# Attention products recorded ahead of the first turned tokens in a fused attention, Fourier and MLP kernel

## The chip, the cores and the metric

The kernel runs on one core of one Trainium2 chip. The metric is the time of one execution on the device in microseconds (us), the median of several runs. All data are float32.

## The reference

Four inputs matter: `q`, `k`, `v` of shape (4, 8, 768, 64), a decay `lam` for each of 8 heads, and two weights of shapes (512, 2048) and (2048, 512). Cut to what matters, the program computes this:

```python
# attention with a decay, in blocks along the sequence, state kv of 64 x 64 for each head
intra = ((qb @ kb.T) * Dmask) @ vb            # Dmask[i,j] = lam**(i-j) for i >= j, else 0
inter = (qb * lam_pow) @ kv
out[block] = intra + inter
kv = lam_block * kv + (kb * rev_pow).T @ vb
# (B,H,S,D) -> (B,S,H*D), then the second half
mixed = real(fft(fft(x, axis=1), axis=2))     # along the sequence and along the width
u = x + mixed
un = (u - mean(u)) / sqrt(var(u) + 1e-6)      # over the width of 512
out = u + maximum(un @ w_ch1, 0) @ w_ch2
```

## The kernel before, in words

The kernel works in chunks of 128 tokens, 6 for each of the 4 batches. Each part of the work is a Python generator that records instructions and yields a number, its estimate of how long they take. The function `beside` weaves two generators: it advances the second one in proportion to what the first has yielded. So the numbers decide in which order instructions are recorded. After that a scheduler of the language orders the instructions of each engine again, by what it takes to be ready and by the recorded order. An instruction handed to `tc.keep_in_program_order` is pinned: it stays behind everything that was recorded before it on its engine.

These are the parts, with the lines that the profile shows:

- `attn(b)` is the attention of one batch, chunk by chunk. `attn_in` loads k, q and v (L263, on the SyncE queue), and turns k and q on TensorE (L274, L279), copied back by ScalarE (L276, L281). VectorE makes `qs`, q times its decay (L285). `attn_out` multiplies k and q (L298), and VectorE applies the decay mask to give `sc` (L302, twice). It then updates the state (L315 to L320, not in the last chunk), adds `qs` times the old state (L328) and `sc` times v (L332) in one accumulation, and copies the result as `oT` (L335). Last, `oT` is turned to tokens (L348) and copied (L352, L353). In the last chunk of batch 1, two gathers of mirrored tokens (`mirror_a`, L439 and L445) are recorded after L302, and two more (`mirror_b`, L452) at its end.
- `fft_ln(b)` does the Fourier mix and the norm of one batch. VectorE folds mirrored rows together (L426 to L484), so that the transforms are products with small cosine and sine tables. TensorE multiplies along the sequence (L516), then along the width (L529 to L534) for three groups of 2 x 128 tokens. ScalarE and VectorE put the results together (L592 to L600; for the first row of one group also L606 to L609). `norm` then takes the statistics (L546, L547 on VectorE; L550, L551 on GpSimd), writes the normalised tokens `un` (L564, two halves for each of two tiles, one buffer), turns them on TensorE (L569) and copies them to `ut` on ScalarE (L570).
- `mlp(b, g, f0, f1)` multiplies `ut` with the first weight (L633), applies the maximum (L639 on VectorE or L641 on ScalarE), multiplies with the second weight (L647), and adds to the tokens (L654, L655 or L658, L659). Four of the twelve groups (`PLAIN`) go this way, three of them in two halves of the hidden width. The others (`late`, L720 to L796) follow at the end with a scheme of seven products in place of eight.
- `weights()` loads weight blocks as raw words (L209, on the SyncE queue, 512 KB each) and turns them into float32 with VectorE and ScalarE passes (L216 to L225). The raw blocks share four buffers with the hidden activations `hr`.

The change sits where batch 0's mix is woven with batch 1's attention and the weights:

```python
run(beside(part(mix, T_FOLD), T_FOLD, att1, 3.25 * t_chunk))
run(beside(mix, 24.0, beside(att1, 2.75 * t_chunk, w, 0.16 * NW), 0.16 * NW + 1.75 * t_chunk))
```

`mix` is `fft_ln(0)`. When `norm` of its first group yields 5.0 after the statistics, the weave advances `att1` and `w` for that long, and then the normalised tokens and their turning are recorded.[...]

## Time and profile before

| | |
|---|---|
| median of 3 runs | 826.14 us (825.62 to 828.82) |
| profiled execution | 824.8 us from the first instruction to the last |
| TensorE busy | 798.2 us (97%) |
| TensorE weight loads | 637.5 us (77%) |
| VectorE busy | 437.8 us (53%) |
| ScalarE busy | 186.5 us (23%) |
| GpSimd busy | 78.4 us (10%) |
| data moved | 68.88 MB |

In the profile PE is TensorE, PEld its weight load, DVE VectorE, ACT ScalarE, POOL GpSimd, and SPq the SyncE queue. A row of a timeline gives start and length in us, the engine, the source line, the operation, output and input tiles with their sizes, and the number of records. In brackets stands how long the engine had been idle before, and what ended that. A product of float32 operands shows as two records. The page divides the span into 40 slices of 20.6 us and gives the busy share of each engine in tenths, and with PEclk the TensorE clock that was granted. The weave with the change runs from 76 to 115 us. It is followed by the first half of the MLP beside the front of batch 1; the seven-product part begins at about 434 us and lasts to the end.

### The profile page before, as it was taken

The page shows a single profiled execution, that of the slowest core. Times are in us where ns is not written, and L with a number is a line of the kernel's source. Part 1 is how long each engine was busy: PE and PEld are TensorE (multiplying, and loading weights), DVE is VectorE, ACT ScalarE, POOL GpSimd, SP SyncE. Part 2 cuts the span into 40 slices and gives each one's busy share as a digit, 9 for nine tenths or more (in the row PEclk, how much of TensorE's full clock was granted, in tenths as well). Part 3 has the DMA queues.
Part 4 walks back from the last instruction along what each step waited for, and adds up shares of the span by engine and source line. Part 5 has one row for each costly group of instructions (what it writes and reads, how often), then busy time and mean ns, then how long its engine had stood idle before and what let it go on. Part 6 is the DMA issues. An engine that isn't in the chain of part 4 may idle for free.

```text
span 824.8 us, 11701 instructions
## 1 busy us (share of the span) xinstructions
PE 798.2 (97%) x4608; PEld 637.5 (77%) x4608; DVE 437.8 (53%) x1018; ACT 186.5 (23%) x448; POOL 78.4 (10%) x102
## 2 busy tenths in 40 slices
PE   7989799999999999999999999999999999999998
PEld 5767675758575857768748888888888888888886
DVE  6899779685745571345895541155313561146311
ACT  3755243324521211212102210022001220012100
POOL 3123310011110110220100000000000000000000
PEclk9999899999999999999999999999999999999999
DMA  9969343238842137530442011100111001110010
GB/s 240 259 132 280 98 152 99 83 75 202 212 116 68 55 74 141 128 120 2 115 115 89 1 52 51 52 1 0 54 50 52 0 1 39 33 33 0 1 39 25
DMA packets 126684, 68.88 MB, mean 84 GB/s; under 512 B 111150, under 2 KB 112174, under 8 KB 126630
## 3 DMA queue, kind: packets, MB, share of 16 engines
q1 hardware_dynamic: 121488, 55.67, 26.6%
q0 software_dynamic: 2112, 6.69, 2.5%
q10 hardware_dynamic: 3030, 5.78, 2.0%
q8 instruction: 36, 0.59, 0.3%
q14 instruction: 18, 0.15, 0.1%
HBM read 48.72 MB, written 19.40 MB: 83 GB/s over the span
## 4 chain that ended last, share of the span: by engine, by line
PE 81%; DVE 9%; issue 4%; DMA 3%; ACT 2%; POOL 1%; POOLq 0%; ACTq 0%; DVEq 0%; SPq 0%
PE p L767 23%; PE p L720 23%; PE pm L647 10%; PE pm L633 8%; PE pa L332 3%; PE pa L298 3%; PE pa L516 3%; PE pa L328 2%; DMA raw<-in_moe_w_ch_dram 2%; PE pa L274 1%; PE pa L315 1%; PE pa L348 1%; PE pa L279 1%; DMA x<-xb,ix 1%; DVE sc L302 1%
## 5 line engine op out<-in xcount | busy, mean ns | idle before, releaser
L633 PE MATMUL pm<-ut,w 128*128 128x256 f32 x512 | 119.9, 383 | 0.0
L647 PE MATMUL pm<-w,hr 128*128 128x512 f32 x256 | 115.8, 597 | 0.6 <-DVE w L225 0.6
L633 PEld LDWEIGHTS pm<-ut,w 128*128 128x128 f32 x512 | 94.2, 190 | 15.8 <-issue 4.1
L720 PE MATMUL p<-ur,w 128*128 128x256 f32 x384 | 93.8, 379 | 0.0
L647 PEld LDWEIGHTS pm<-w,hr 128*128 128x128 f32 x256 | 46.7, 190 | 50.0 <-issue 47.8
L720 PEld LDWEIGHTS p<-ur,w 128*128 128x128 f32 x384 | 73.0, 190 | 10.3 <-issue 0.5
L720 PE MATMUL p<-us,w1s 128*128 128x256 f32 x256 | 65.7, 379 | 0.0
L767 PE MATMUL p<-w,hs 128*128 128x256 f32 x256 | 58.0, 379 | 0.5 <-DVE y L788 0.5
L767 PE MATMUL p<-w2s,hs 128*128 128x256 f32 x256 | 57.9, 379 | 0.0
L767 PE MATMUL p<-w,ha 128*128 128x256 f32 x256 | 57.9, 379 | 0.0
L767 PEld LDWEIGHTS p<-w,hs 128*128 128x128 f32 x256 | 48.5, 190 | 7.5 <-DVE y L788 0.9
L767 PEld LDWEIGHTS p<-w2s,hs 128*128 128x128 f32 x256 | 48.6, 190 | 6.6
L767 PEld LDWEIGHTS p<-w,ha 128*128 128x128 f32 x256 | 48.6, 190 | 6.6
L720 PEld LDWEIGHTS p<-us,w1s 128*128 128x128 f32 x256 | 48.6, 190 | 6.6
L747 ACT COPY ha<-p 128x256 f32<-128x256 f32 x32 | 11.9, 372 | 169.1 <-PE p L720 139.4
L622 POOL DMA_INDIRECT out_dram<-y,ix x12 | 11.8, 988 | 402.4 <-DVE y L793 341.6
L758 DVE TENSOR_TENSOR ha<-p,ha 128x256 f32<-128x256 f32 x32 | 13.6, 425 | 45.2 <-ACT ha L757 45.2
L298 PEld LDWEIGHTS pa<-qT,kT 64*128 64x128 f32 x384 | 26.8, 198 | 12.8 <-ACT qT L281 6.7
L302 DVE TENSOR_TENSOR sc<-pa,decay 128x512 f32<-128x512 f32 x48 | 31.5, 683 | 8.2 <-PE pa L298 8.2
L332 PE MATMUL pa<-sc,v 128*64 128x128 f32 x384 | 32.3, 286 | 3.1 <-DVE sc L302 3.0
L298 PE MATMUL pa<-qT,kT 64*128 64x128 f32 x384 | 31.5, 297 | 2.9 <-ACT qT L281 2.6
L720 PE MATMUL p<-us,w 128*128 128x256 f32 x128 | 32.9, 379 | 0.0
(144 smaller groups left out, 1122.1 us busy)
## 6 DMA issues: line engine op xcount, KB each, us to landing
raw<-in_moe_w_ch_dram SPq DMA_DIRECT2D x32, 512.0 KB, 4.6
k<-in_k_dram SPq DMA_DIRECT2D x24, 256.0 KB, 5.0
q<-in_q_dram SPq DMA_DIRECT2D x24, 256.0 KB, 5.9
v<-in_v_dram SPq DMA_DIRECT2D x24, 256.0 KB, 4.9
ud<-x SPq DMA_DIRECT2D x16, 256.0 KB, 2.3
utd<-e SPq DMA_DIRECT2D x64, 64.0 KB, 2.2
u<-ud SPq DMA_DIRECT2D x16, 256.0 KB, 2.7
ur<-utd SPq DMA_DIRECT2D x6, 512.0 KB, 4.4
```

The costliest lines, as they stand in the source:

```text
L298: mm(pss[hi][:, hp, :], lhsT=kT[HD[hi], hp, :], rhs=qT[HD[hi], hp, :], start=True, stop=True)
L302: nc.vector.tensor_tensor(t, pss[hi], decay[:, hi::2, :], op=ALU.mult)
L328: mm(po[HD[hi], hp, :], lhsT=s_old[HD[hi], hp, :], rhs=qs[HD[hi], hp, :], start=(hp == 0), stop=False, skip_group_check=True)
L332: mm(po[HD[hi], hp, :], lhsT=vt[:, 2 * hp + hi, :], rhs=sc[hi][:, hp, :], start=(c == 0 and hp == 0), stop=(hp == HP - 1), skip_group_chec ...
L516: mm = nc.tensor.matmul(ps[0:m, n, :], lhsT=piece(a, i, n), rhs=cs[0:rows, a, i in (2, 3), n, :], start=(a == 0), stop=(a == 1))
L622: nc.gpsimd.indirect_dma_start(out=out.rearrange("b s d -> (b s) d"), out_offset=row_of(2 + HC * (b + 1) + T - HC), in_=y[:, :], in_offset ...
L633: nc.tensor.matmul(ps, lhsT=w1[:, c, 128 * fc:128 * fc + 128], rhs=ut[:, c, :], start=(c == 0), stop=(c == KO - 1))
L647: nc.tensor.matmul(ps, lhsT=hr[(fc - f0) // 4][:, fc % 4, 128 * i:128 * i + 128], rhs=w2[:, fc, :], start=(fc == f0), stop=(fc == f1 - 1))
L720: nc.tensor.matmul(ps, lhsT=s2.A[a][:, kt, 128 * i:128 * i + 128], rhs=U[b][:, kt, :], start=(first and kt == 0), stop=(kt == 1), skip_gro ...
L747: nc.scalar.copy(a11, two(X))
L758: V.tensor_tensor(a22, two(Z), a22, op=ADD)
L767: nc.tensor.matmul(ps, lhsT=h[a][:, s, i, :], rhs=s2.B[b][:, i, :], start=(first and i == 0), stop=(i == HF - 1), skip_group_check=True)
```

## The change

Two edits, both in `norm` and both for the first group of batch 0, `PLAIN[0]`. The number yielded after the statistics becomes 9.0, so that more of batch 1's attention is recorded between the statistics and the tokens. And the very first turning product is pinned on TensorE behind all that was recorded before it, so that the scheduler doesn't move it ahead of these attention products. It is meant to give TensorE the attention's products while VectorE and GpSimd work on the norm.

```diff
-            yield 5.0 if (b, g) == PLAIN[0] else 1.0
+            yield 9.0 if (b, g) == PLAIN[0] else 1.0
...
                 if plain:
                     pt = psum_a([128, KO, 128])
                     for c in range(KO):
-                        nc.tensor.transpose(pt[:, c, :], un[:, 128 * c:128 * c + 128], ident)
+                        mm = nc.tensor.transpose(pt[:, c, :], un[:, 128 * c:128 * c + 128], ident)
+                        if (b, g, i, c) == (*PLAIN[0], 0, 0):
+
+                            tc.keep_in_program_order(mm)
                     nc.scalar.copy(ut[:, :, 128 * i:128 * i + 128], pt)
```

Lines behind the first edit keep their numbers; those behind the second are three higher in the changed kernel (L633 becomes L636).

## The prediction

> **What bounds the kernel now.** I read the page's busy shares and slices first, then the table of stretches around the one dip, the timelines of TensorE, VectorE and the SyncE queue there, and last the waits of TensorE after it.

> ```profile
> PE   7989799999999999999999999999999999999998
> PEclk9999899999999999999999999999999999999999
> ```
> TensorE is the bound nearly everywhere. The fifth slice (82 to 103 us) is the only one in which the granted clock falls.

> ```profile
> 88.00:92.00 4.00, 0.26 (x3) 0.02 (x1) 3.07 (x8) 1.05 (x4) 1.29 (x2) 1.00 1.09 245
> 92.00:96.00 4.00, 2.94 (x13) 2.57 (x14) 2.06 (x5) 0.86 (x2) 1.66 (x2) 0.52 0.26 87
> 96.00:100.00 4.00, 4.00 (x37) 3.65 (x38) 2.00 (x5) 0.81 (x4) 1.48 (x2) 0.63 0.55 162
> ```
> Columns: stretch, then busy time of TensorE, weight load, VectorE, ScalarE, GpSimd, then granted clock. TensorE does nothing for most of 88 to 92, and is granted half its clock just after.

> ```profile
> 87.66 0.60 PE L348 MATMUL pa<-ident,oT 128*128 128x128 f32 x4
> 92.55 1.09 PE L569 MATMUL pa<-ident,un 128*128 128x128 f32 x4 [4.29 <-DVE un L564]
> 94.15 0.69 PE L569 MATMUL pa<-ident,un 128*128 128x128 f32 x2 [0.51 <-DVE un L564]
> 97.33 1.93 PE L298 MATMUL pa<-qT,kT 64*128 64x128 f32 x16
> 99.19 1.09 PE L328 MATMUL pa<-qs,st 64*64 64x128 f32 x16
> 102.26 1.09 PE L332 MATMUL pa<-sc,v 128*64 128x128 f32 x14
> 115.12 0.67 PE L569 MATMUL pa<-ident,un 128*128 128x128 f32 x4 [0.43 <-DVE un L564]
> 135.14 1.12 PE L647 MATMUL pm<-w,hr 128*128 128x512 f32 x2 [0.56 <-DVE w L225]
> ```
> The turned tokens (L569) wait 4.29 us for the first normalised tokens. The attention products of the last chunk of batch 1 (L298, L328, L332) stand behind them, although their inputs were there.

> ```profile
> 89.75 0.65 DVE L285 TENSOR_TENSOR qs<-pa,qpow 128x512 f32<-128x512 f32 x1
> 90.42 0.65 DVE L224 SCALAR_TENSOR_TENSOR w<-raw,w 128x512 f32<-128x512 uint32 x1
> 91.99 0.74 DVE L564 TENSOR_SCALAR un<-x,mv,rs 128x256 f32<-128x256 f32 x2 [0.93 <-POOL rs L551]
> 97.97 0.43 DVE L596 TENSOR_TENSOR ds<-pa,bs 128x256 f32<-128x256 f32 x1 [3.56 <-ACT bs L592]
> ```
> ```profile
> 103.38 0.37 SPq L263 DMA_DIRECT2D v<-in_v_dram  x1
> 103.85 1.04 SPq L209 DMA_DIRECT2D raw<-in_moe_w_ch_dram  x2
> 115.97 0.33 SPq L209 DMA_DIRECT2D raw<-in_moe_w_ch_dram  x1
> ```
> VectorE idles 3.56 us because TensorE is late. The load of v waits for L332 to free its buffer, and the raw weights (L209) queue behind that load.

> ```profile
> PE pa L516 <- DVE fe L475: 2.2, 3, 1.0
> PE pa L332 <- DVE sc L302: 1.6, 1, 1.6
> PE p L767 <- DVE y L788: 0.5, 1, 0.5
> ```
> These are all of TensorE's named waits from 160 us to the end: 4.3 us. What TensorE gains before 150 us should therefore reach the end.

> [...]

> **The change part by part.** In the changed program's instruction order only TensorE, VectorE and ScalarE differ, and only between the rows that ran at 88 and about 146 us. No instruction is added or removed. TensorE: L298, L328 and L332 now stand before L569, and L348 (turning oT) before the first L633. VectorE: both L302 and one L225 stand before the first L564, and some weight and fold work (L217 to L225, L426 to L430) moves up from after 112 us. The two edits of the diff (9.0 for 5.0, and the pin) bring about one order; I cost that order. I replay it with durations of this trace at full clock; spacings back to back are 0.60 us for a 512-wide VectorE pass, 0.34 for a 256-wide one, and 0.44 for one L633 product (two records of 0.22).

> 1. *The gap.* qT is ready at 88.49 (copy of 0.59 from 87.90). L298 runs 88.6 to 89.8 (1.16 in its full-clock rows, against 1.93 here). L328 waits for qs, 90.40, and runs 90.5 to 91.6. On VectorE L224 ends its slot at 91.02; L302 twice, to 92.3. L332 starts on the first at 91.8, waits for the second at 92.4, and is done by 93.4. So 3.3 us of products (1.16 + 1.09 + 1.09) go into the 4.29 us gap, in pieces: the idle spells are 0.3, 0.75, 0.2 and 0.4 us.
> 2. *What is put behind.* L564 follows L302 and L225: 91.02 + 1.20 + 0.60 = 92.8 instead of 91.99, so the first L569 goes at 93.4 instead of 92.55, about when L332 ends. Queued behind the added waits on TensorE are these transposes; VectorE's second L564, ScalarE's ut copies and all of the first group's norm wait for them. That is a loss of 0.85 us, and the only one I find.
> 3. *The clock.* [...] Between 48 and 52 us TensorE was busy 3.02 of 4.00 and kept its clock. I take full clock; then L569 and L529 to L534 run at 0.22 us a product, not 0.43. The second un starts at 94.1, its transposes at 94.7, L534 ends at 96.3, L348 at 96.6, and L633 starts at 96.6. In the trace L348 and the products up to 103.28 without three L633 stand at 103.28 + 0.44 - 1.3 = 102.4. TensorE is 5.8 us ahead there. Of this 2.7 us are clock (0.5 + 0.3 + 0.2 on the transposes, 5 x 0.21 on L529 to L534, 0.77 on L298, rounded), the rest the filled gap.
> 4. *The next norm.* The VectorE chain starts at 96.9 instead of 97.97 and no longer holds L302 (1.2 us): L596 to L600, 1.9; L546 and L547, 1.5; GpSimd's two, 1.2. So L564 starts at 101.5 instead of 103.83. TensorE has ten L633 (4.4 us) until 101.0, then waits 1.1 us for L569, where before it waited for nothing. After L530 to L532 it is 105.7 us with 12 L633 done; in the trace 108.81 with 8. Lead: 3.1 + 4 x 0.44 = 4.9 us.
> 5. *VectorE until 135.* Here VectorE limits: from 108.3 it idles 1.1 us until 135. Its idle spells from 90 to 135 sum to 10.2 us (0.93, 0.35, 3.56, 1.17, 0.76, 2.26, 0.92, 0.22). In the replay they sum to 5.3 (0.6, 2.0, 1.2, 0.4, 0.3, 0.6, 0.2). It can use that time because v and the raw weights behind it are issued at 93.5 and 94.0 instead of 103.38 and 103.85; a raw block landed 4.4 us after its issue at 115.97, so both are in by 102 even beside the gathers. The third raw block follows the first L224, at 104.7 instead of 115.97. Two short passes (0.67) move behind the third block's L225, which ends at 135.08 - 4.9 - 0.67 = 129.5.
> 6. *Down products.* L647 starts at 116.1 instead of 121.10; its 28 records and two L633 take it to 129.0; it waits for L225 until 129.6 instead of 135.14. One L633 moved behind it: lead 5.6 - 0.4 = 5.2 us.
> 7. *The gathers.* L352 waits for L609 and its successors: 110.7 instead of 111.95. With the same 7 us to the landed gather (issue 112.63, first L452 at 114.96, landing 3.7 us later) the fold's input is in at 117.7, wanted at 118.4. This is hidden by 0.7 us.

> From there the order is the old one and TensorE has next to no waits: 826.14 - 5.2 = 820.9 us.

> **The rivals.** *A: the clock still falls,*[...]. For: the pieces fill only about 60% of 88 to 94. Against: 48 to 52 us. Then the 2.7 us of step 3 are lost: gain 2.5, 823.6 us; a late fold (step 7) or a weight wait gives about the same. *B: VectorE gives it all back.* For: L647 waits for L225 already, and VectorE is busy without a break from 115 to 135. If the raw blocks don't come earlier, L225 stays at 135.08 and the time at 826. Against: their only blocker in the queue is v's buffer, which L332 frees. *C: slower.* The pin puts the first norm behind L332, and the clock falls under it: +0.85 of step 2, and 1.8 us more for L298, L328 and L332 at half clock before the transposes, 828.8 us. For: the norm is a chain, and the chain of waits runs through it. Against: TensorE would still have done 3.3 us of work that it now does later.

> **How the numbers follow.** Forecast (gain 4 to 6.5): 0.74. A: 0.14. B: 0.06. C: 0.06. Half a per cent is 4.1 us; nearly all of the forecast lies above it, some just below: faster 0.70, same 0.24, slower 0.06. The range runs from 819.0 (the whole 5.8 us and half of the 2.3 us of waits that steps 4 and 1 leave) to 824.3, past A; B, C and the tails make up the rest.

> **What would show it.** Right: L569 starts near 93.4 with a short wait; the clock is 1.00 in 92 to 100; v is issued near 93.5; TensorE waits about 1.1 us before the second norm's L569; the last pair of L647 waits for L225 near 129.6; after 150 us everything is about 5 us earlier. Wrong: a clock near 0.5 after 92; L225 of the third block after 131; L426 waiting for the second gather for more than a us; or a lead at 150 us that is gone at the end.

## The result, and the profile after

The changed kernel takes 821.45 us (median of 6 runs, 820.58 to 823.3), the kernel before beside it 825.81 us (6 runs, 825.07 to 828.82). The ratio is 0.9945, with a 95% interval of 0.9927 to 0.9962: a gain of 4.4 us by the medians. A second series gave 822.27 against 826.99 us (ratio 0.996, 0.9941 to 0.9979). The profiled execution spans 819.4 us, before 824.8.

The page's slices of the changed kernel, busy share and granted clock:

```profile
PE   6989899999999999999999999999999999999998
PEclk9999999999999999999999999999999999999999
```

The fifth digit of PEclk, the only low one before, is now 9. The table of stretches, with the columns in the order of before (TensorE, weight load, VectorE, ScalarE, GpSimd, then the granted clock, the busy share of the DMA engines and GB/s; `pa` and `pm` in the rows that follow are the kernel's two pools of buffers for products, `pa` of the attention and the mix, `pm` of the MLP):

```profile
88.00:92.00 4.00, 2.82 (x36) 2.15 (x38) 4.00 (x10) 0.59 (x3) 1.30 (x2) 1.00 1.20 283
92.00:96.00 4.00, 3.49 (x34) 2.97 (x33) 2.03 (x5) 1.78 (x4) 2.15 (x2) 1.00 0.58 149
96.00:100.00 4.00, 4.00 (x22) 3.56 (x21) 3.45 (x8) 0.99 (x5) 0.99 (x1) 1.00 0.95 319
```

TensorE works 2.82 us of the first stretch, where it worked 0.26, and the clock stays at 1.00 where it was 0.52 and 0.63. The timeline of TensorE in the changed kernel:

```profile
87.20 0.60 PE L348 MATMUL pa<-ident,oT 128*128 128x128 f32 x4
88.09 1.16 PE L298 MATMUL pa<-qT,kT 64*128 64x128 f32 x16 [0.29 <-ACT qT L281]
90.00 1.09 PE L328 MATMUL pa<-qs,st 64*64 64x128 f32 x16 [0.75 <-DVE qs L285]
91.26 0.43 PE L332 MATMUL pa<-sc,v 128*64 128x128 f32 x2 [0.17 <-DVE sc L302]
91.86 1.09 PE L332 MATMUL pa<-sc,v 128*64 128x128 f32 x14 [0.17 <-DVE sc L302]
92.88 0.67 PE L569 MATMUL pa<-ident,un 128*128 128x128 f32 x4
...
101.74 0.67 PE L569 MATMUL pa<-ident,un 128*128 128x128 f32 x4 [1.04 <-DVE un L564]
...
129.40 1.12 PE L650 MATMUL pm<-w,hr 128*128 128x512 f32 x2 [0.17 <-DVE w L225]
...
147.63 0.76 PE L569 MATMUL pa<-ident,un 128*128 128x128 f32 x4 [0.94 <-DVE un L564]
```

The wait of 4.29 us is gone. In its place stand the three products with short waits, and the first turned tokens go out behind them without any. The same kernel's VectorE and SyncE queue:

```profile
92.33 0.73 DVE L564 TENSOR_SCALAR un<-x,mv,rs 128x256 f32<-128x256 f32 x2
96.52 0.43 DVE L599 TENSOR_TENSOR ds<-pa,bs 128x256 f32<-128x256 f32 x1 [1.96 <-ACT ds L598]
128.66 0.68 DVE L225 SCALAR_TENSOR_TENSOR w<-w,e 128x512 f32<-128x512 f32 x1
```

```profile
92.98 0.37 SPq L263 DMA_DIRECT2D v<-in_v_dram  x1
93.45 11.54 SPq L209 DMA_DIRECT2D raw<-in_moe_w_ch_dram  x3
```

VectorE's longest wait has fallen from 3.56 to 1.96 us, and v and the raw weights leave some 10 us earlier. The third raw block of that row is issued at 104.66, before at 115.97. TensorE's named waits from 155 us to the end are those of before:

```profile
PE pa L516 <- DVE fe L475: 2.1, 3, 1.0
PE pa L332 <- DVE sc L302: 1.6, 1, 1.6
PE p L770 <- DVE y L791: 0.5, 1, 0.5
```

**How the gain is measured from here on.** Up to the turning of oT (L348) both kernels do the same work, but this row starts anywhere between 86.8 and 90.5 us in the profiles below. In four of them the clock fell to 0.50 for 3.4 us before it, at about 28 us in e1, e5 and e8 and at 72.5 us in e7, and these have the four latest starts (88.90 to 90.53 us, the others 86.76 to 88.75). The rest of this spread stays open. So I also count from the start of L348 to the start of the next norm's first L569, and to the end of the span. These rows of before are needed for that:

```profile
101.27 0.43 PE L332 MATMUL pa<-sc,v 128*64 128x128 f32 x2
152.94 0.76 PE L569 MATMUL pa<-ident,un 128*128 128x128 f32 x4 [0.94 <-DVE un L564]
```

Before: 152.94 - 87.66 = 65.28 us, and 824.8 - 87.66 = 737.1 us. After: 147.63 - 87.20 = 60.43 us, a lead of 4.85, and 819.4 - 87.20 = 732.2 us, a lead of 4.9. The second series' profile gives 4.98 and 5.0. What is gained by 148 us is there at the end. Counted so, profiles of one order agree to 0.2 us (e7, which has the order of before, gives 65.10 and 737.0), unless the clock falls elsewhere.

### The profile page after: what moved, and what is told of

The parts are those of the page before. It is cut to its first block, busy times and chain, and to the rows that moved or that the text cites. A ratio compares the mean times of both kernels' runs of the same rounds, so it can differ in the third digit from the quotient of the medians.

```text
span 819.4 us, 11694 instructions
## 1 busy us (share of the span) xinstructions
PE 795.2 (97%) x4608; PEld 634.9 (77%) x4608; DVE 437.8 (53%) x1018; ACT 186.5 (23%) x448; POOL 86.1 (11%) x102
## 4 chain that ended last, share of the span: by engine, by line
PE 80%; DVE 10%; issue 4%; DMA 3%; ACT 2%; POOL 1%; POOLq 0%; ACTq 0%; DVEq 0%
PE p L770 24%; PE p L723 24%; PE pm L650 10%; PE pm L636 8%; PE pa L332 3%; PE pa L516 3%; PE pa L298 3%; DMA x<-xb,ix 2%; PE pa L328 2%; PE pa L274 1%; DVE sc L302 1%; PE pa L315 1%; PE pa L348 1%; PE pa L279 1%; DVE stt L546 1%
## 5 line engine op out<-in xcount | busy, mean ns | idle before, releaser
L636 PE MATMUL pm<-ut,w 128*128 128x256 f32 x512 | 119.2, 382 | 0.0
L650 PE MATMUL pm<-w,hr 128*128 128x512 f32 x256 | 115.8, 597 | 0.2 <-DVE w L225 0.2
L636 PEld LDWEIGHTS pm<-ut,w 128*128 128x128 f32 x512 | 94.4, 190 | 15.4 <-issue 3.6
L650 PEld LDWEIGHTS pm<-w,hr 128*128 128x128 f32 x256 | 46.6, 190 | 49.5 <-issue 48.0
L298 PEld LDWEIGHTS pa<-qT,kT 64*128 64x128 f32 x384 | 26.0, 193 | 13.2 <-ACT qT L281 7.3
L302 DVE TENSOR_TENSOR sc<-pa,decay 128x512 f32<-128x512 f32 x48 | 31.5, 683 | 8.8 <-PE pa L298 8.5
L332 PE MATMUL pa<-sc,v 128*64 128x128 f32 x384 | 32.1, 284 | 4.1 <-DVE sc L302 4.1
L298 PE MATMUL pa<-qT,kT 64*128 64x128 f32 x384 | 30.7, 292 | 3.2 <-ACT qT L281 2.9
L270 POOL TENSOR_TENSOR kd<-k,decay 128x512 f32<-128x512 f32 x20 | 23.0, 1152 | 94.8 <-PE pa L315 64.5
```

Source lines behind the costliest of these rows:

```text
L270: nc.gpsimd.tensor_tensor(kd, kt, kpow, op=ALU.mult)
L298: mm(pss[hi][:, hp, :], lhsT=kT[HD[hi], hp, :], rhs=qT[HD[hi], hp, :], start=True, stop=True)
L302: nc.vector.tensor_tensor(t, pss[hi], decay[:, hi::2, :], op=ALU.mult)
L332: mm(po[HD[hi], hp, :], lhsT=vt[:, 2 * hp + hi, :], rhs=sc[hi][:, hp, :], start=(c == 0 and hp == 0), stop=(hp == HP - 1), skip_group_chec ...
L636: nc.tensor.matmul(ps, lhsT=w1[:, c, 128 * fc:128 * fc + 128], rhs=ut[:, c, :], start=(c == 0), stop=(c == KO - 1))
L650: nc.tensor.matmul(ps, lhsT=hr[(fc - f0) // 4][:, fc % 4, 128 * i:128 * i + 128], rhs=w2[:, fc, :], start=(fc == f0), stop=(fc == f1 - 1))
```

## The experiments

Leads are against the profile of before, counted from L348 as above. Inserted lines shift the line numbers of what follows (L569 is L574 in e1 to e3, L576 in e6 and e9; in e6 L222, L643 and L651 are L216, L633 and L641 of before). An execution's mean granted clock is on record too: one fall of 3.4 us to half the clock takes 0.002 from it by my estimate (3.4 x 0.5 of 825 us; e1's profiled execution, with one such fall, has 0.998).

**Which edit does it?** e4 has the number alone, e7 the pin alone.

```diff
e4
-            yield 5.0 if (b, g) == PLAIN[0] else 1.0
+            yield 9.0 if (b, g) == PLAIN[0] else 1.0
e7
-                        nc.tensor.transpose(pt[:, c, :], un[:, 128 * c:128 * c + 128], ident)
+                        mm = nc.tensor.transpose(pt[:, c, :], un[:, 128 * c:128 * c + 128], ident)
+                        if (b, g, i, c) == (*PLAIN[0], 0, 0):
+                            tc.keep_in_program_order(mm)
```

> The change without its pin: 9.0 is yielded, nothing is pinned. The instruction order of every engine comes out as that of the changed kernel. Theory: the yield alone carries the gain, 821.4 us, within 0.2% of the changed kernel, with the same 0.29, 0.75 and 0.17 us waits in the gap. Rival (the pin matters): the time lies between the two kernels.

> The pin alone, with 5.0 yielded as before. The instruction order of every engine is that of the kernel before, so the time should be that of before, 825.8 us, within 0.2%, with the 4.29 us wait and the clock of 0.5 after it.

e4 took 822.11 us (ratio 0.9942, 0.9925 to 0.996), with the waits of the changed kernel and a lead of 5.0 us at the end. e7 took 826.63 us (ratio 1.0004, 0.9996 to 1.0013), with the wait of 4.29 us and clocks of 0.62 and 0.52. The order of instructions on every engine is that of the changed kernel in e4, and that of before in e7. The yielded number does all of it.

**How much is the clock?** e1 to e3 keep the order of before and put work that nobody reads into the gap: four products of 128x512, thirty transposes of the identity, or one product.

```diff
+            if (b, g) == PLAIN[0]:
+                junk = psum_m([128, DM])
+                for n in range(4):          # e2: range(30), e3: range(1)
+                    tc.keep_in_program_order(
+                        nc.tensor.matmul(junk, lhsT=ident, rhs=decay[:, 0:4, :], start=True, stop=True))
e2
+                        nc.tensor.transpose(junk[:, 128 * (n % 4):128 * (n % 4) + 128], ident, ident))
```

> The kernel before, with four added TensorE products of 128x512 (3.4 us at 0.43 us a record) that nobody reads, pinned between the turning of oT and the first turned tokens; the order of everything else is that of before. Theory (2.7 us of the gain is the clock, the rest is useful work put into the gap): the granted clock stays at 1.00 from 92 to 100 us, L534 ends about 2 us earlier, and the time falls by 2 to 2.7 us, to about 823.4, half of what the change brings. Rival 1 (the gain is the filled gap alone): the time stays within 0.5 us of before. Rival 2 (it is all the clock): it falls by 4 us or more.

> As the run with products in the gap, but with 30 transposes of the identity (0.11 us each, 3.3 us) in their place. If transposes keep the clock up as products do, the time and the clock are those of that run (about 823.4, 1.00). If they don't count as activity, the clock falls to about 0.5 after 92 us and the time stays at about 825.8.

> As the first run, with a single product of 128x512 (0.87 us) at the head of the gap, so that some 3.3 us of idleness are left before the first turned tokens. If an idle spell of 3.3 us is short enough, the clock stays at 1.00 and the time is about 823.4; if not, the clock falls as before and the time is about 825.8. The first is a little likelier.

The stretches of e1, then TensorE's timeline there:

```profile
92.00:96.00 4.00, 3.13 (x10) 1.18 (x9) 3.07 (x9) 0.00 (x0) 1.30 (x2) 1.00 1.13 268
96.00:100.00 4.00, 3.49 (x42) 3.14 (x42) 1.89 (x6) 1.67 (x5) 2.62 (x3) 1.00 0.20 68
```

```profile
90.53 0.60 PE L348 MATMUL pa<-ident,oT 128*128 128x128 f32 x4
90.97 3.60 PE L559 MATMUL pm<-decay,ident 128*128 128x512 f32 x8
95.44 0.67 PE L574 MATMUL pa<-ident,un 128*128 128x128 f32 x4 [0.87 <-DVE un L569]
...
101.70 0.43 PE L332 MATMUL pa<-sc,v 128*64 128x128 f32 x2
```

With 3.6 us of idle work in the gap the clock stays at 1.00. The first turned tokens start 4.91 us after L348, as before (92.55 - 87.66 = 4.89), so up to there nothing but the clock is seen to differ. L332 starts 11.17 us after L348, before 101.27 - 87.66 = 13.61: the clock is worth 2.4 us there. At the next norm the lead is 2.0 us, and at the end 2.0 us. By the times e1 is 825.61 against 827.06 us (ratio 0.9986, 0.9973 to 0.9999), 1.5 us where 2 to 2.7 were expected. In its profile and in others of its 22 executions the clock fell somewhere else. The thirteen with a mean clock of 0.999 or 1 have a median of 825.0, 2.1 us below before, whose executions never come above 0.998.

e2, with transposes alone, does the same to the clock:

```profile
88.00:92.00 4.00, 2.97 (x28) 2.70 (x26) 3.07 (x9) 0.15 (x1) 1.30 (x2) 1.00 1.13 279
92.00:96.00 4.00, 3.49 (x39) 3.01 (x40) 1.89 (x6) 1.67 (x5) 2.47 (x3) 1.00 0.19 59
```

Its lead is 2.4 us at L332 and 2.1 at the next norm, but only 0.4 at the end: in its profile a fold at 371.62 us made TensorE wait 1.56 us (L516 for L475), which it doesn't do in the others. The gather behind this fold (L452) went out at 363.27, still 2.1 us ahead of before counted from L348, but VectorE took up its data 5.0 us later, in before 3.3 us later. Why it was slow is not known. The time is 826.83 us (ratio 0.9994, 0.9977 to 1.0011), no gain that can be told, against the 823.4 expected. Ten of the 14 executions have a mean clock of 0.999 or 1, and even their median is 826.2, so something other than the clock costs e2 about a us against e1.

e3 leaves 3.44 us idle. The wait and the stretches:

```profile
92.82 0.67 PE L574 MATMUL pa<-ident,un 128*128 128x128 f32 x4 [3.44 <-DVE un L569]
92.00:96.00 4.00, 2.67 (x16) 2.41 (x17) 2.01 (x5) 1.17 (x2) 1.83 (x3) 0.81 0.26 98
96.00:100.00 4.00, 4.00 (x39) 3.43 (x39) 2.56 (x5) 0.50 (x3) 1.58 (x2) 0.76 0.57 169
```

The clock falls, where I had held the opposite to be a little likelier. In this profile it falls later and for less long than before, and the lead is 1.1 us. But its mean clock of 0.998 is that of only three of the 14 executions, the others have 0.994 to 0.996, as before mostly has, and the time is 826.85 us (ratio 1.0005, 0.9994 to 1.0017).

**How many of the products are needed?** e5 yields 7.0, which puts only L298 into the gap; e8 yields 11.0. Both keep the pin.

```diff
-            yield 9.0 if (b, g) == PLAIN[0] else 1.0
+            yield 7.0 if (b, g) == PLAIN[0] else 1.0      # e8: 11.0
```

> The changed kernel with 7.0 in place of 9.0: only L298 (1.16 us) goes into the gap, L328 and L332 stay behind the first turned tokens. Theory: TensorE idles about 2.7 us at a stretch, the clock stays at 1.00, and the lead is the clock's 2.7 us and about 1 us of filled gap: 822 us. Rival (the clock falls at this spell too): about 825.

> The changed kernel with 11.0 in place of 9.0: the turning of oT (L348) also moves up, between the first group's turned tokens, and one more L633 product stands before the second group's, which waited 1.04 us. Theory: at most that product's 0.4 us is won, 821 us, not to be told from the changed kernel. Rival (later turned tokens delay the norm): slower by up to 1 us.

e5's wait and stretches:

```profile
95.01 0.67 PE L569 MATMUL pa<-ident,un 128*128 128x128 f32 x4 [3.03 <-DVE un L564]
96.00:100.00 4.00, 3.72 (x24) 3.52 (x26) 0.84 (x4) 1.40 (x5) 3.14 (x3) 0.60 0.30 82
100.00:104.00 4.00, 4.00 (x37) 3.40 (x34) 3.08 (x8) 0.95 (x2) 0.79 (x3) 0.97 0.65 153
```

An idle spell of 3.03 us cost the clock as well, against the theory of 822 us. The lead is 2.8 us at the end, the time 825.24 against 826.49 us (ratio 0.9984, 0.997 to 0.9997), only 1.3 us. The profile lost its clock once in the gap and once at 28 us, before the count begins; where the second loss falls in the other executions, most of which have a mean clock of 0.994 to 0.997, is not on record. So L328 and L332 in the gap are worth another 2.1 us by these profiles and some 3 by the times, by the work moved and by the clock kept. e8 puts L348 between the turned tokens. Its lead is 5.3 at the next norm and 5.2 at the end, and its time 821.61 us (ratio 0.9945, 0.9929 to 0.9961): the same as the changed kernel as far as this can tell.

**Do the weights have to be early?** e6 and e9 are the changed kernel with the raw blocks held back until the second group's first `ut` is there. A small transfer that reads it goes ahead of them in the queue. In e6 it has 128 pieces of 4 bytes, in e9 one row of 512.

```diff
+        calls.append(0)
+        if len(calls) == 14:
+            mark = dram.tile([128, 1], F32, name="mark")          # e9: [1, 128]
+            tc.keep_in_program_order(nc.sync.dma_start(mark, uts[PLAIN[1]][:, 0, 0:1]))   # e9: [0:1, 0, 0:128]
-        nc.sync.dma_start(raw, src.bitcast(U32))
+        i = nc.sync.dma_start(raw, src.bitcast(U32))
+        if len(calls) == 14:
+            tc.keep_in_program_order(i)
...
+    calls = []
```

> The changed kernel, with the 14th raw weight block (the first that is issued at 93.45 us) and those behind it kept back by a tiny transfer that reads the second group's turned tokens, so that they are issued near 103 us as in the kernel before. The scheduler then leaves the fold and weight passes later on VectorE. Theory (the lead reaches the end only because the weights come early and VectorE can use its idle time): the third raw block's L225 ends near 133 instead of 129.3, the last pair of L647 waits 3 to 4 us for it, and the time rises by 2 to 3 us over the changed kernel, to about 823.5 to 824. Rival (TensorE's lead carries by itself): within 0.5 us of the changed kernel.

> The changed kernel with the pair of raw weight blocks held back once more, behind a transfer of one row of 512 bytes that reads the first ut of the second group (in e6 the transfer had 128 pieces of 4 bytes, took 8.4 us to land, and the weights landed behind it at about 116 us). Nothing of the computation is left out. Step 5 as forecast (VectorE needs the weights early): the blocks are issued near 104 and land near 108.5 instead of about 98, VectorE and ScalarE take the weight passes up after 109, L225 of the third block ends 2 to 4 us later than the 129.3 of the changed kernel, and the time is 2 to 4 us above it, 823.5 to 825.5. Rival (the gain comes from TensorE alone and VectorE has the room anyway): the time is within 0.7 us of the changed kernel.

> The changed kernel once more, on the chip of e9, to have its time beside it: ratio to the kernel before 0.9945, as measured, 0.993 to 0.996. Both theories expect the same of this run.

e6 took 831.64 us (ratio 1.0066, 1.0048 to 1.0084), much more than before, and for another reason than the one tried. ScalarE, then TensorE:

```profile
116.68 0.67 ACT L222 ACTIVATE e<-raw 128x512 bf16<-128x512 int16 x1 [9.84 <-DMA raw<-in_moe_w_ch_dram]
117.25 0.36 ACT L651 ACTIVATE hr<-pm 128x256 f32<-128x256 f32 x1
```

```profile
117.67 1.22 PE L643 MATMUL pm<-ut,w 128*128 128x256 f32 x2 [5.28 <-ACT hr L651]
```

The blocks were issued at 104.92, but the small transfer ahead of them took 8.4 us to land, and they landed behind it. ScalarE waited 9.84 us for them with a pass that writes `hr` (L651) queued behind, and TensorE waited 5.28 us for that pass. The clock then fell as well, from 115 to 125 us (0.89 over the stretch from 112 to 116). e6 thus shows what the chain can cost, not what early weights are worth.

e9 shows that. Its blocks were issued at 104.43 and taken up at 108. VectorE and TensorE there (L231 is L225, L657 is L650):

```profile
131.91 0.68 DVE L231 SCALAR_TENSOR_TENSOR w<-w,e 128x512 f32<-128x512 f32 x1
```

```profile
88.28 0.60 PE L355 MATMUL pa<-ident,oT 128*128 128x128 f32 x4
...
132.64 1.12 PE L657 MATMUL pm<-w,hr 128*128 128x512 f32 x2 [1.59 <-DVE w L231]
...
150.01 0.76 PE L576 MATMUL pa<-ident,un 128*128 128x128 f32 x4 [0.94 <-DVE un L571]
```

The last pair starts 44.36 us after L355 (the turning of oT), in e10 42.07: 2.3 us later, with a wait of 1.59 instead of 0.16. At the next norm 1.4 us of that are left (61.73 against 60.30). The times are 824.05 and 822.27 us, 1.8 apart, though the intervals of their ratios overlap (0.9948 to 0.9978, 0.9941 to 0.9979). Executions with a mean clock of 0.999 or 1 don't overlap: four of e9 at 823.4 to 824.1, four of e10 at 821.7 to 822.3, 2.0 apart by their medians. (e9's profile is its slowest execution. It is only 1.0 us ahead of before at the end, because the clock fell at 298 us.) Of some 5 us, 1.4 to 2.0 therefore hang on the weights being early. That is at or below the low end of the 2 to 4 expected, and more than the rival's 0.7. The scheduler also ordered VectorE's and ScalarE's passes anew in e9, the results of the mix ahead of the weight passes, which may have made the delay milder.

## Why the prediction was right, point by point

The forecast was 820.9 us, a gain of 5.2; measured were 4.4 us by the medians and 4.9 by the lead. The case that came is the likeliest one. Times of the replay are on the clock of before, so 0.46 us (87.66 - 87.20) is added to the rows of after.

1. *The gap.* Right, though the reading ahead of it was loose: of the three products only L298 had its inputs when the wait began, L328 and L332 had to wait for `qs` and `sc`. L298, L328 and both L332 start at 88.55, 90.46, 91.72 and 92.32 on that clock (forecast 88.6, 90.5, 91.8, 92.4). The waits are 0.29, 0.75, 0.17 and 0.17 (0.3, 0.75, 0.2, 0.4).
2. *What is put behind.* Right: the first L569 at 93.34 instead of 92.55, a loss of 0.8 (0.85).
3. *The clock.* Right that it stays, and the size nearly: 2.7 us forecast (the terms listed add up to 2.8), 2.4 measured at L332 by e1 and e2, of which 2.0 reach the end in e1. The other 2.9 us of the lead (4.9 - 2.0) are put down to the filled gap by subtraction. That it stays was an estimate of mine, from the one stretch of 48 to 52 us (busy 3.02 of 4.00). Short idle spells alone would not have been a safe ground, since one of 3.03 us cost the clock in e5, and at 28 us in e1 it fell after spells of 1.23 and 1.21 us. In the changed kernel TensorE works at least 66% of any 3.41 us there, and in the twelve traces no such window above 54% ended with a fall (last section). The forecast didn't look at that, and was lucky in it.
4. *The next norm.* Right: TensorE waits 1.04 us (1.1). The L636 after L530 to L532 starts at 105.97, 0.3 later than the forecast 105.7. The forecast of the later rows is too early by the same few tenths.
5. *VectorE until 135.* Right. v and the raw blocks are issued at 93.44 and 93.91 (93.5, 94.0). VectorE's idle spells sum to 5.3 us (0.53, 1.96, 1.17, 0.53, 0.93, 0.18), as forecast. L225 of the third block ends at 129.80 (129.5). e9 shows that the early blocks matter: without them L225 ends 2.2 us later from L348.
6. *Down products.* L650's last pair waits for L225 at the place foreseen and starts at 129.86 (129.6). The next norm's L569 comes at 148.09, where the forecast lead of 5.2 puts it at 147.74. These tenths of steps 4 to 6 are what the forecast of the gain has too much.
7. *The gathers.* The first fold of gathered rows (L426) starts at 118.78 without a wait, as forecast (118.4). The second gather, which I had not timed, is 0.18 us late for its fold at 123.94.

The low end of the range has a slip: the idle spells of steps 1 and 4 add up to 2.75 us, not 2.3. Half of that gives the 819.0 that stands there.

**The rivals.** A, the fallen clock, did not come: 1.00 throughout. It was a real danger for a smaller change, since in e5 it took away part of the gain. Neither transposes nor 64-row products cost the clock here: with thirty transposes in the gap of e2, 3.44 us, it was 1.00 as with the products of e1, 3.60 us. The 64-row products L298 and L328 are most of what TensorE does from 88.1 to 91.1 us in the changed kernel, and the clock stayed at 1.00. B, VectorE giving all back, holds for a part: with late blocks (e9) 1.4 to 2.0 us go, not all five. C, slower, did not come: L569 is 0.8 us later and never runs at the low clock.

## What to carry to other kernels

Where an engine waits for a chain on others and ready work stands behind the waiting instruction, record that work ahead: on TensorE this paid twice here, by the time filled (2.9 us) and by the clock kept (2.0). For the clock, look at how much of every 3.4 us TensorE works, not at the longest idle spell: below half it fell each time here (7 windows of 7), and a filling that left a spell of 3.03 us lost it all the same. Then follow what the moved products release (here a buffer, and through it the loads queued behind), because about a third of the gain hung on that, and replay each engine's order with the trace's own durations.

## What the runs showed of the hardware that was not expected

| TensorE busy in the window | windows, twelve traces | ended with a fall |
|---|---|---|
| under 50% | 7 | 7 |
| 50 to 54% | 15 | 3 |
| over 54% | 2798 | 0 |

Before has 0% from 88.73 to 92.15 us, e3 34% from 91.07 to 94.49, e5 35% from 93.38 to 96.80. In e1 the window from 24.81 to 28.23 has 39%, with no spell over 1.23 us. So the fall can come after the work has resumed: in e3 at 94.49 us, 1.7 us after the first turned tokens at 92.82. A low spell lasts whole windows, one in e3 and two in the gap of before, and each ended after a window that was busy throughout.

The experiments fit this. Slide a window of 3.41 us over the traces: in the gap of before, e3 and e5 every position of the grid leaves one window below half (the best positions leave 32, 42 and 42%). In the changed kernel no position gives less than 66%, in e1 60%, in e2 55%. The mean clocks agree: 0 of 90 executions of before, 0 of 14 of e3 and 0 of 22 of e5 are above 0.998, but 12 of 19 of the changed kernel (with e4 and e10), 13 of 22 of e1 and 10 of 14 of e2. In e2 the window from 86.80 to 90.21 us holds nothing but transposes, and the clock stayed at 1.00.

Near one half the windows went both ways (3 of 15 ended with a fall). In e9's profiled execution the clock fell far from the change, in a window of 53.5% behind a wait of 1.59 us that ends at 297.34:

```profile
296.00:298.00 2.00, 0.66 (x5) 0.49 (x5) 2.00 (x6) 0.00 (x0) 1.87 (x3) 1.00 0.38 65
298.00:300.00 2.00, 2.00 (x17) 1.52 (x15) 0.22 (x1) 0.00 (x0) 0.62 (x1) 0.57 0.38 66
300.00:302.00 2.00, 2.00 (x8) 1.61 (x8) 0.00 (x0) 1.66 (x3) 0.00 (x0) 0.58 0.00 0
```

The same wait in before, e1 and e10 lies in windows of 53 to 54% and left the clock at 1.00; what tips such a window was not tried.

**A scattered small transfer.** In e6 a transfer of 512 bytes in 128 pieces of 4 bytes, issued at 104.49, took 8.4 us to land, while the DMA engines were busy throughout (share 1.04) at only 27 GB/s from 104 to 108 us. The raw blocks issued behind it at 104.92 were taken up at 116.68. In e9 the same bytes as one row held nothing up: the blocks landed 4.0 us after their issue, in the changed kernel 4.1.
